# Two batches of a feed-forward network put behind attention as seven block products, with q/k copies on GpSimd and half of the output evictions on ScalarE

## The chip, the core and the metric

The kernel runs on one core of a Trainium2 chip. The metric is the device time of one execution in microseconds. Before the change it is 324.69 us, the median of three runs (324.67 to 325.06). One more execution was taken with the hardware profiler; its span, from the first to the last instruction, is 322.9 us, and TensorE's granted clock was 1.000 throughout.

The engines are named as the profile names them: PE is TensorE (matrix products), PEld its loading of weights, DVE is VectorE, ACT is ScalarE, POOL is GpSimd, SP is the engine that mostly issues transfers. Each engine works through its own queue in order, and an instruction that must wait holds up what stands behind it on that queue. SBUF is the on-chip memory that all engines work on; PSUM holds the results of matrix products, in eight banks of 512 float32 columns for each of 128 partitions.

## What is computed

Attention with one extra term in the softmax's denominator, over 8 batches, 12 heads, 448 positions and a head size of 64, and behind it a feed-forward network with three up-projections, of which the elementwise maximum is taken:

```python
def _attn_ref(q, k, v):                       # each (8, 12, 448, 64)
    scale = 1.0 / np.sqrt(q.shape[-1])
    scores = scale * np.matmul(q, k.transpose(0, 1, 3, 2))
    m = np.max(scores, axis=-1, keepdims=True)
    e = np.exp(scores - m)
    attn = e / (np.sum(e, axis=-1, keepdims=True) + np.exp(-m) + 1e-09)
    return np.matmul(attn, v)

def _moe_ref(x, w1, w2, w3, w_out):           # x (3584, 768), weights (768, 768)
    h = np.maximum(np.maximum(x @ w1, x @ w2), x @ w3)
    return h @ w_out
```

x is attention's result with the heads of one position side by side, so each of its 3584 rows belongs to one position of one batch.

## The kernel before

**Attention.** The 12 heads of a batch are taken in three groups of four, which makes 24 groups, numbered 0 to 23. In a group, four heads lie in the four 64x64 quarters of TensorE and are worked on side by side, so four matmuls of 64x64 run in the time of one. One group is

- seven "score" units (`visit`): four matmuls of 448 columns each into a pair of PSUM banks (tile "stp"), then one exponential on ScalarE over 896 columns into tile "eT";
- six additions on VectorE that sum the exponentials of the seven units (`sum_e`, tile "eS");
- one denominator (`den_group`): four matmuls with ones, then a logarithm on ScalarE into "lnd", and `recip_group`, an exponential of its negative into "rb";
- one product with v (`num_group`): 28 matmuls into a pair of banks (tile "av"), and `norm_group`, two multiplications on VectorE that write x transposed into the tile "xT" of the batch.

Three pairs of PSUM banks are shared in turn by scores, denominator and products in the early part; two in the later part.

**Loads and transposes.** GpSimd issues the loads of q, k and v, and in the later part each load waits for a score matmul so that loads are spread (`load_behind`). TensorE needs q and k transposed. For groups 0 to 7 it transposes them itself. From group 8 on, two VectorE copies (`copy_qk`, line 190) bring k and q of group i+2 into one tile "qk16", and one transposing transfer on SP's queue (`dma_transpose`) makes "qkT".

**Feed-forward.** It is cut into pieces. An up piece (`up_piece`) is one of 6 column blocks of one of 3 up-projections for one batch: 6 sets of four matmuls of 64x64 by 448 columns (line 758). VectorE then copies the result to "hT" (first projection) or takes the maximum with what is there. An output piece (`out_piece`) is one of 7 tiles of 128 rows of two batches, and one of 2 halves of 384 columns: 6 sets by 384 columns; VectorE scales it into an output tile "o_sb" (line 542), and after the second half two stores go out on SP's queue, 192 KB each. The batches' pieces stand in a list; `step` issues the next set, up to three pieces being worked on together, in a ring of four single PSUM banks.

**Order.** From group 7 on the order of TensorE's work is written out: for each group a list (`ORDER`) of score units (U), denominator (D) and product (N) with a weight each, and after every item so many `step`s as `rate` and the weight say. `batch_done(b)` adds the pieces of batch b once its x is there and sets the rate. The last four pieces are held back each time (`HELD`) to fill the stretch until the next batch is ready. A piece is taken up only when what it reads is written. After group 23 what is left of the pieces is worked off, which here is a good part of batches 6 and 7.

Names that the prediction's steps use: "set" is four matmuls of 64x64 side by side; "group 22" is the last but one; "the first av group" is the first whose product stands as 28 matmuls on line 322, "the last" is group 23's.

Of the kernel before, what the change touches and what calls it, by code (L numbers as in the profile page):

```python
# [10 lines left out]
FP32 = mybir.dt.float32  # L11
FP16 = mybir.dt.float16
AF = mybir.ActivationFunctionType
ALU = mybir.AluOpType
# [8 lines left out]
def kernel(  # L23
# [33 lines left out]
    )  # L57

    cpool = ctx.enter_context(tc.tile_pool(name="const", bufs=1))
    ld_pool = ctx.enter_context(tc.tile_pool(name="ld", bufs=5))  # L60
    p16_pool = ctx.enter_context(tc.tile_pool(name="p16", bufs=3))
    att_pool = ctx.enter_context(tc.tile_pool(name="att", bufs=4))
    e_pool = ctx.enter_context(tc.tile_pool(name="e", bufs=3))
    small = ctx.enter_context(tc.tile_pool(name="small", bufs=2))
    xt_pool = ctx.enter_context(tc.tile_pool(name="xt", bufs=2))
    ht_pool = ctx.enter_context(tc.tile_pool(name="ht", bufs=2))
    out_pool = ctx.enter_context(tc.tile_pool(name="outp", bufs=6))

    ps1 = ctx.enter_context(tc.tile_pool(name="ps1", bufs=2, space=bass.MemoryType.PSUM))
    ps2 = ctx.enter_context(tc.tile_pool(name="ps2", bufs=1, space=bass.MemoryType.PSUM))
    third = ExitStack()
    ps3 = third.enter_context(tc.tile_pool(name="ps3", bufs=1, space=bass.MemoryType.PSUM))
    turn = [0]
# [61 lines left out]
            reason="spreads the loads",  # L137
        )

    first_k = cpool.tile([128, 2, NJ, D], FP32, name="first_k")  # L140
    load_half(nc.sync, first_k, "k", 0, 0)
    load_half(nc.scalar, first_k, "k", 0, 1)
    load_group(0, "q")
# [22 lines left out]
                )  # L166
    w_sb = [cpool.tile([128, NDC, DFF], MMDT, name=f"w{i}") for i in range(4)]
    wout_sb = w_sb[3]


    def load_weight(i, f0=0, f1=DFF):
# [14 lines left out]
    def copy_qk(i, n):  # L186
        st = state.setdefault(i, {})
        if n == 0:
            st["qk16"] = p16_pool.tile([128, 2, NJ, 2, D], MMDT, tag="qk16", name="qk16")
        nc.vector.tensor_copy(  # L190
            out=st["qk16"][:, n].rearrange("p j s d -> p s j d"), in_=raw[i]["kq"[n]]
        )

# [43 lines left out]


    def first_group():
        k16 = p16_pool.tile([128, NJ, 2, D], MMDT, tag="k16", name="k16", bufs=1)  # L240
        qkT = att_pool.tile([128, 2, NJ, 128], MMDT, tag="qkT", name="qkT")
        state[0] = {"qkT": qkT}
        cuts = (((0, 4), (0, 3)), ((4, NJ), (3, NJ)))
        for (k0, k1), _ in cuts:
            nc.vector.tensor_copy(
                out=k16[:, k0:k1].rearrange("p j s d -> p s j d"), in_=first_k[:, :, k0:k1]
            )
        for (k0, k1), (q0, q1) in cuts:
            nk = k1 - k0
            trT = single("trT", (NJ, 128), MMDT)  # L250
            for j in range(k0, k1):
                nc.tensor.transpose(
                    out=trT[:, j - k0, :], in_=k16[:, j].rearrange("p s d -> p (s d)"),
                    identity=ident16,
                )
            for j in range(q0, q1):
                transpose_slots(trT[:, nk + j - q0, :], raw[0]["q"][:, :, j])
            nc.vector.tensor_copy(out=qkT[:, 0, k0:k1], in_=trT[:, 0:nk])
            nc.vector.tensor_copy(out=qkT[:, 1, q0:q1], in_=trT[:, nk:NJ])
# [70 lines left out]
    def den_group(i):  # L330
        st = state[i]
        dps = double("den")
        av_tiles(
            [dps[:, r, 0:S] for r in range(2)],
            lambda r, c: ones16[half(r)],
            lambda r, c: st["eS"][half(r), c],
            True,
            True,
        )
        st["lnd"] = small.tile([128, 2, S], FP32, tag="lnd", name="lnd")  # L340
        nc.scalar.activation(  # L341
            out=st["lnd"], in_=dps[:, :, 0:S], func=AF.Ln, bias=1.0 / EDIV
        )

    def recip_group(i):
        st = state[i]
        st["rb"] = small.tile([128, 2, S], FP32, tag="rb", name="rb")
        nc.scalar.activation(  # L348
            out=st["rb"], in_=st.pop("lnd"), func=AF.Exp, bias=math.log(LAMBDA), scale=-1.0
        )  # L350

    def num_group(i, in_pair=True):
# [66 lines left out]
    def den_part(i, part):  # L419
        st = state[i]  # L420
        q0, q1 = PARTS[part]
        nq = (q1 - q0) * KC
        eT = st["eT", part]
        dps = double("den")
        terms = [eT[:, j] for j in range(NJ)]
        if "eP" in st:
            eP, n = st.pop("eP")
            terms = [eP[:, 0], eP[:, 1]] + terms[n:]
        for n, e in enumerate(terms):
            av_tiles(  # L430
                [dps[:, r, 0:nq] for r in range(2)],
                lambda r, c: ones16[half(r)],
                lambda r, c: e[half(r), c],
                n == 0,
                n == len(terms) - 1,
            )
        lnd = small.tile([128, 2, S], FP32, tag="lnd", name="lnd")
        nc.scalar.activation(
            out=lnd[:, :, 0:nq], in_=dps[:, :, 0:nq], func=AF.Ln, bias=1.0 / EDIV
        )  # L440
        rb = small.tile([128, 2, S], FP32, tag="rb", name="rb")
        nc.scalar.activation(
            out=rb[:, :, 0:nq], in_=lnd[:, :, 0:nq], func=AF.Exp, bias=math.log(LAMBDA), scale=-1.0
        )
        st["rb", part] = rb

# [80 lines left out]
    def out_piece(bp, t, nh, bank=None, done=False):  # L527
        if nh == 0:
            outs[0] = out_pool.tile([128, DM], FP32, tag="o_sb", name="o_sb")
        o_sb = outs[0]  # L530
        op_ps = single("op_ps") if bank is None else bank
        for fc in range(0 if done else NFC):
            nc.tensor.matmul(  # L533
                out=op_ps[:, 0:NW],
                lhsT=hT[bp][:, fc, ts(t, 128)],
                rhs=wout_sb[:, fc, ts(nh, NW)],
                start=(fc == 0),
                stop=(fc == NFC - 1),
            )
        last = bp == B // 2 - 1 and t == NT - 1  # L540
        cut = nh * NW + (NW // 2 if last and nh == NH - 1 else NW)
        nc.vector.tensor_scalar(  # L542
            out=o_sb[:, nh * NW : cut],
            in0=op_ps[:, 0 : cut - nh * NW],
            scalar1=1.0 / LAMBDA,
            scalar2=None,
            op0=ALU.mult,
        )
        if cut < nh * NW + NW:
            nc.scalar.activation(  # L550
                out=o_sb[:, cut:DM], in_=op_ps[:, NW // 2 : NW], func=AF.Copy, scale=1.0 / LAMBDA
            )
        if last or nh == NH - 1:
            cols = ts(nh, NW) if last else slice(0, DM)
            for n in range(2):
                b, j = divmod(2 * t + n, NJ)
                b += 2 * bp
                rows = out[b * S : (b + 1) * S].rearrange("(p j) m -> j p m", j=NJ)
                eng = nc.scalar if last and n == 1 else nc.sync
                eng.dma_start(out=rows[j][:, cols], in_=o_sb[half(n), cols])  # L560
# [8 lines left out]
    def add_ups(b):  # L569
        for fc in range(NFC):  # L570
            for i in range(3):
                pieces.append((up_piece, (b, fc, i), NDC * (S + 6)))
# [132 lines left out]

    third.close()
    flush()
    single_pools.append(ctx.enter_context(tc.tile_pool(name="ps4", bufs=2, space=bass.MemoryType.PSUM)))
    pair_pools.pop()
    LAG = 2  # L710
    flow = []
# [126 lines left out]
    TOTAL = sum(w for _, _, w in ORDER)  # L838


    def batch_done(b):
        add_ups(b)
        last_batch[0] = b == B - 1
        pieces.extend(held)
        held.clear()
        add_out(b, *((0, 3) if b % 2 == 0 else (3, 7)))
        if b < B - 1:
            held.extend(pieces[-HELD:])
            del pieces[-HELD:]
        rate[0] = (left() - (SPARE if b < B - 2 else LAST)) / 3  # L850

    SPARE, LAST = 30, 50
    rate = [0]
    batch_done(1)
    after(9, sum_e, MID, 1)
    after(14, sum_e, MID, 2)
# [3 lines left out]
    for i in range(MID, NI + 1):  # L860
        for op, j, w in ORDER if i > MID else ORDER[4:]:
            if op == "U" and i < NI:
                mm = visit([(i, j)])
                n, name = ((2, "v"), (3, "k"), (3, "q"), (0, ""))[j // 2]
                if n > 0 and i + n < NI and i > MID:
                    load_behind(mm, i + n, name, j % 2)
                steps[0] += 1
                if j == 2:
                    recip_group(i - 1)
                if j > 0:  # L870
                    after({1: 9, 2: 14, 3: 20, 4: 9, 5: 9, 6: 9}[j], sum_e, i, j)
                if j == (9 if i == 7 else 3) and PE_TR <= i + 2 < NI:
                    for n_ in range(2):
                        copy_qk(i + 2, n_)
                    dma_transpose(i + 2)
# [16 lines left out]
            steps_for(rate[0] * w / TOTAL if i < NI else (8 if op == "D" else 0))  # L892
    while late or left() or count[1] < count[0]:
        step()


# [28 lines left out]
```

## Time and profile before

| | us |
|---|---|
| median of three runs | 324.69 |
| span of the profiled execution | 322.9 |
| TensorE busy | 308.2 (95%) |
| VectorE busy | 235.3 (73%) |
| ScalarE busy | 191.7 (59%) |
| GpSimd busy | 96.8 (30%) |
| feed-forward matmuls, line 758 | 246.0 in all |
| score exponentials, line 299, 147 of them | 132.8, 0.916 each |
| additions of exponentials, line 308, 126 of them | 78.0, 0.619 each |
| q/k copies, line 190, 32 of them | 12.4, 0.387 each |
| output evictions, line 542, 56 of them | 29.7, 0.550 each |
| end of the last attention product | 274.8 |
| end of the last matmul | 317.4 |

The busy time of TensorE is no measure of its limit: matmuls overlap, and a matmul that waits inside the pipeline counts as busy. So the number of matmuls between two points in the program's order, each at the time that undisturbed ones take, is set against the time that the trace shows between these points. The chain of waits, which follows the execution back from its end, is read in order of time: each line has the start in us, its length, the engine or transfer, the tile, the line and a count. In the groups of instructions the columns are: line, engine, operation, output<-input with partitions x columns and type, count | busy us, mean ns of one | idle time before them and what ended it. In the timeline they are: start, length, engine, line, operation, count, and in brackets the idle time before it.

### The profile page before, as it was taken

The numbers are of one execution on the slowest core, as the hardware profiler recorded it, in microseconds if no ns is written. First come the engines' busy times: TensorE is split into PE (matmuls) and PEld (weight loads), VectorE is DVE, ScalarE is ACT, GpSimd is POOL, SyncE is SP. The second block draws the span as 40 slices with busy tenths as digits, with TensorE's granted clock in tenths as the row PEclk, the third lists the DMA queues.
The fourth block names the chain that finished last, engine by engine and source line by source line (L and its number), as shares of the span: only waits on it lengthen the run. The fifth ranks groups of instructions, "written<-read, shape, count | busy, mean of one in ns | idle before, by whom it ended". The sixth has DMA issues, their size and how long they took to land.

```text
span 322.9 us, 14605 instructions
## 1 busy us (share of the span) xinstructions
PE 308.2 (95%) x6607; PEld 260.1 (81%) x6607; DVE 235.3 (73%) x443; ACT 191.7 (59%) x227; POOL 96.8 (30%) x166
## 2 busy tenths in 40 slices
PE   7669998999999999999999999999999999999993
PEld 6557676658998899988889877897787788887892
DVE  3446598998887878777769688878778777645652
ACT  2898859887786565575575685685576674000000
POOL 8947565840433132232222232232220000000000
PEclk9999999999999999999999999999999999999999
DMA  7999999999877975779969997899966500050046
GB/s 143 165 191 186 190 190 188 163 159 185 119 98 105 197 135 94 116 147 163 76 99 150 198 150 111 103 179 157 92 81 124 136 4 2 2 150 2 2 122 175
DMA packets 59517, 40.75 MB, mean 126 GB/s; under 512 B 32704, under 2 KB 56000, under 8 KB 59456
## 3 DMA queue, kind: packets, MB, share of 16 engines
q0 software_dynamic: 25344, 21.01, 48.1%
q1 hardware_dynamic: 33808, 18.39, 28.3%
q8 instruction: 51, 0.84, 1.1%
q10 hardware_dynamic: 304, 0.43, 0.5%
q14 instruction: 10, 0.08, 0.1%
HBM read 42.47 MB, written 11.01 MB: 166 GB/s over the span
## 4 chain that ended last, share of the span: by engine, by line
PE 79%; DMA 14%; POOL 3%; issue 1%; DVE 1%; ACT 0%; ACTq 0%; DVEq 0%; POOLq 0%
PE piece L758 59%; PE av L322 9%; PE stp L276 8%; DMA w<-in_moe_w_dram 7%; DMA ld_q<-in_q_dram 4%; DMA w<-in_moe_w_out_dram 2%; PE piece L533 2%; PE den L322 1%; PE piece L510 1%; DMA out_dram<-o_sb 1%; POOL w L180 1%; POOL w L181 1%; POOL ld_v L111 1%; POOL ld_q L111 1%; DVE eS L308 0%
## 5 line engine op out<-in xcount | busy, mean ns | idle before, releaser
L758 PE MATMUL piece<-xT,w 64*64 64x448 f16 x3024 | 177.7, 349 | 0.3 <-DVE xT L375 0.3
L299 ACT ACTIVATE eT<-stp 128x896 f16<-128x896 f32 x147 | 132.8, 916 | 65.9 <-PE stp L276 63.3
L758 PEld LDWEIGHTS <-w 64*64 64x64 f16 x3024 | 132.1, 107 | 21.2 <-issue 1.6
L276 PE MATMUL stp<-qkT 64*64 64x448 f16 (+2 forms) x756 | 71.3, 331 | 2.4 <-ACT eTp L394 0.8
L758 PE MATMUL piece<-w,hT 64*64 64x384 f16 x1224 | 68.3, 323 | 0.0
L308 DVE TENSOR_TENSOR eS<-eS,eT 128x896 f16<-128x896 f16 x105 | 65.0, 619 | 2.7 <-DVE eS L308 0.5
L499 DVE TENSOR_TENSOR hT<-hT,piece 128x448 f16<-128x448 f16 x84 | 51.9, 618 | 19.8 <-PE piece L758 16.8
L758 PEld LDWEIGHTS <-hT 64*64 64x64 f16 x1224 | 53.6, 107 | 4.4 <-issue 0.7
L111 POOL DMA_DIRECT2D ld_q<-in_q_dram x48 | 28.9, 606 | 60.3 <-PE piece L758 33.9
L111 POOL DMA_DIRECT2D ld_v<-in_v_dram x48 | 28.5, 599 | 47.7 <-PE stp L276 30.1
L276 PEld LDWEIGHTS <-qkT 64*64 64x64 f16 x756 | 32.1, 106 | 10.2 <-issue 5.5
L542 DVE TENSOR_SCALAR o_sb<-piece 128x384 f32<-128x384 f32 (+1 forms) x56 | 29.7, 550 | 13.4 <-PE piece L758 12.8
L497 DVE CAST hT<-piece 128x448 f16<-128x448 f32 x42 | 26.1, 621 | 14.4 <-PE piece L758 13.8
L111 POOL DMA_DIRECT2D ld_k<-in_k_dram x46 | 27.7, 609 | 27.5 <-PE piece L758 12.0
L322 PE MATMUL av<-eT,ld_v 64*64 64x448 f16 x588 | 33.3, 349 | 0.0
L322 PEld LDWEIGHTS <-ld_v 64*64 64x64 f16 x756 | 28.7, 107 | 4.2 <-issue 0.2
L375 DVE TENSOR_TENSOR xT<-av,rb 128x448 f16<-128x448 f32 x42 | 24.3, 619 | 9.0 <-PE av L322 8.8
L550 ACT ACTIVATE o_sb<-piece 128x192 f32<-128x192 f32 x1 | 0.3, 330 | 44.6 <-DMA out_dram<-o_sb 44.6
L510 PEld LDWEIGHTS <-w 128*128 128x128 f16 x216 | 18.8, 98 | 6.2 <-issue 4.1
L341 ACT ACTIVATE lnd<-den 128x896 f32<-128x896 f32 x21 | 19.3, 917 | 7.2 <-PE den L322 6.6
L394 ACT ACTIVATE eTp<-stp 128x768 f16<-128x768 f32 (+3 forms) x24 | 18.0, 821 | 7.1 <-PE stp L276 7.1
L348 ACT ACTIVATE rb<-lnd 128x896 f32<-128x896 f32 x21 | 20.0, 951 | 0.2
(50 smaller groups left out, 158.0 us busy)
## 6 DMA issues: line engine op xcount, KB each, us to landing
out_dram<-o_sb SPq DMA_DIRECT2D x54, 192.0 KB, 4.0
ld_q<-in_q_dram POOLq DMA_DIRECT2D x48, 112.0 KB, 4.3
ld_v<-in_v_dram POOLq DMA_DIRECT2D x48, 112.0 KB, 3.8
ld_k<-in_k_dram POOLq DMA_DIRECT2D x46, 112.0 KB, 4.2
w<-in_moe_w_dram POOLq DMA_DIRECT2D x6, 192.0 KB, 6.7
w<-in_moe_w_out_dram POOLq DMA_DIRECT2D x3, 384.0 KB, 7.6
w<-in_moe_w_dram POOLq DMA_DIRECT2D x2, 384.0 KB, 6.2
w<-in_moe_w_dram POOLq DMA_DIRECT2D x1, 576.0 KB, 8.3
```

Source lines behind the costliest of these rows:

```text
L111: return eng.dma_start(out=dst[hp * KC : hp * KC + KC].rearrange("p s j d -> p s (j d)"), in_=src[:, half_heads(name, hp)],)
L276: mm = nc.tensor.matmul(out=out[half(c), r], lhsT=qkT[half(r), 0, j, h], rhs=qkT[half(r), 1, q0:q1, h], start=True, stop=True,)
L299: nc.scalar.activation(out=st["eT"][:, j], in_=stp[:, :, 0:S], func=AF.Exp, scale=scale, bias=-math.log(EDIV))
L308: nc.vector.tensor_tensor(out=st["eS"], in0=st["eT"][:, 0] if j == 1 else st["eS"], in1=st["eT"][:, j], op=ALU.add,)
L322: nc.tensor.matmul(out=outs[r][half(c)], lhsT=weights(r, c), rhs=moving(r, c), start=start, stop=stop,)
L348: nc.scalar.activation(out=st["rb"], in_=st.pop("lnd"), func=AF.Exp, bias=math.log(LAMBDA), scale=-1.0)
L375: nc.vector.tensor_tensor(out=xT[b][:, 2 * g + r, :], in0=banks[r][:, 0:S], in1=state[i]["rb"][:, r], op=ALU.mult)
L497: nc.vector.tensor_copy(out=dst, in_=p_i[:, 0:S])
L499: nc.vector.tensor_tensor(out=dst, in0=dst, in1=p_i[:, 0:S], op=ALU.max)
L510: nc.tensor.matmul(out=p_i[:, ts(j, nq)], lhsT=w_sb[i][:, dc, ts(2 * fp + j, 128)], rhs=xT[b][:, dc, q0 * KC : q1 * KC], start=(dc == 0), ...
L542: nc.vector.tensor_scalar(out=o_sb[:, nh * NW : cut], in0=op_ps[:, 0 : cut - nh * NW], scalar1=1.0 / LAMBDA, scalar2=None, op0=ALU.mult,)
L758: nc.tensor.matmul(out=p["bank"][half(c), 0:w], lhsT=lhs(k, r, c), rhs=rhs(k, r), start=(r == p["first"] and k == 0), stop=(r != p["first" ...
```

## The change

- The pieces of batches 6 and 7 are no longer in the list. `batch_done` now handles batches 0 to 5 (`LATE = B - 2`), and the rate spreads what is left of them over all groups to come, but for 30 sets.
- When attention and those pieces are done, the pools of attention and all PSUM banks are given back, and a tail begins with eight single banks and full 128x128 matmuls. The two batches' rows and the halves of the contraction form 2x2 blocks, and so do each weight's halves. Each up-projection (9 units: 3 projections x 3 column blocks) and each output unit (3 units) is made of seven block products of three matmuls each, p1 to p7, in place of eight. Products accumulate in two banks, "a" and "s", and ScalarE copies or VectorE additions take intermediate sums out between them. The seventh tile of 128 rows of the pair, and four held pieces, are computed as before (`plain`).
- The block sums of the weights ("comb", four for each weight, 1152 columns) are subtractions on GpSimd: those of the first weight at the start of group 22, the others behind attention. The block sums of x ("sx", 1344 columns) and of h ("sh", 1152 columns) are four VectorE operations each.
- The q/k copies from group 11 on are on GpSimd.
- Half of the output evictions (the second 384 columns) are on ScalarE, but for the last tile.
- The logarithm is written straight into "rb" and the exponential is taken in place; the first k tiles come from the pool of "qk16"; "xT" has four buffers, not two, and "o_sb" five, not six.

```diff
-        nc.vector.tensor_copy(
+        eng = nc.gpsimd if i > 10 else nc.vector
+        eng.tensor_copy(
             out=st["qk16"][:, n].rearrange("p j s d -> p s j d"), in_=raw[i]["kq"[n]]
         )
...
-        nc.vector.tensor_scalar(
-            out=o_sb[:, nh * NW : cut],
...
+        if nh == 0 or last:
+            nc.vector.tensor_scalar(
+                out=o_sb[:, nh * NW : cut],
...
+        else:
+            nc.scalar.activation(
+                out=o_sb[:, NW:DM], in_=op_ps[:, 0:NW], func=AF.Copy, scale=1.0 / LAMBDA
+            )
...
+    LATE = B - 2
     def batch_done(b):
-        add_ups(b)
-        last_batch[0] = b == B - 1
...
+        if b < LATE:
+            add_ups(b)
+            last_batch[0] = b == LATE - 1
...
-        rate[0] = (left() - (SPARE if b < B - 2 else LAST)) / 3
+        coming = sum(NFC * 3 + (6 if x % 2 == 0 else 8) for x in range(b + 1, LATE))
+        steps_left = left() + NDC * (coming + (len(held) if b < LATE - 1 else 0))
+        rate[0] = (steps_left - LAST) / max(NI - max(3 * b + 3, MID) - 0.4, 1)
+    LAST = 30
...
+    def combine_weight(i):
+        w, t, m = w_sb[i], comb[i], DFF // 2
+        sub = ALU.subtract
+        b11, b12 = w[:, 0:3, 0:m], w[:, 0:3, m:DFF]
+        b21, b22 = w[:, 3:6, 0:m], w[:, 3:6, m:DFF]
+        for out_, in0, in1 in ((0, b12, b11), (1, b22, t[:, 0]), (2, b22, b12), (3, b21, t[:, 1])):
+            nc.gpsimd.tensor_tensor(out=t[:, out_], in0=in0, in1=in1, op=sub)
...
+                if j == 1 and i == NI - 2:
+                    combine_weight(0)
...
+    banks.close()
+    att.close()
+    tail = ctx.enter_context(tc.tile_pool(name="tail", bufs=1))
+    tps = ctx.enter_context(tc.tile_pool(name="tps", bufs=8, space=bass.MemoryType.PSUM))
+    for i in range(1, 4):
+        comb[i] = tail.tile([128, 4, 3, DFF // 2], MMDT, name=f"comb{i}")
+        combine_weight(i)
...
+    def combine_moving(name, a11, a12, a21, a22, n):
+        s = tail.tile([128, 4, 3, n], MMDT, name=name)
+        sub, add = ALU.subtract, ALU.add
+        for out_, in0, in1, op in (
+            (0, a21, a22, add),
+            (1, s[:, 0], a11, sub),
+            (2, a11, a21, sub),
+            (3, a12, s[:, 1], sub),
+        ):
+            nc.vector.tensor_tensor(out=s[:, out_], in0=in0, in1=in1, op=op)
+        return s
+    sx = combine_moving("sx", x1[:, 0:3], x1[:, 3:6], x2[:, 0:3], x2[:, 3:6], S)
...
+        def put(b, fc, out_of, bank, other=None):
+            dst = h_of[b][:, fc]
+            if other is None and i == 0:
+                nc.scalar.activation(out=dst, in_=bank, func=AF.Copy)
+            elif other is None:
+                nc.vector.tensor_tensor(out=dst, in0=dst, in1=bank, op=ALU.max)
+            elif i == 0:
+                nc.vector.tensor_tensor(out=dst, in0=other, in1=bank, op=ALU.add)
+            else:
+                nc.vector.tensor_tensor(out=out_of, in0=other, in1=bank, op=ALU.add)
...
+        def p1():
+            bank_of(u, "a")
+            copy("p1", product(u, "a", lambda k: w[:, k, c0], lambda k: x1[:, k], S, True))
+        def p2():
+            bank_of(u, "s")
+            bank = product(u, "s", lambda k: w[:, 3 + k, c0], lambda k: x1[:, 3 + k], S, True)
+            u["c"] = tail.tile([128, 3, S], MMDT, tag="c", name="c", bufs=3)
+            put(0, f, u["c"][:, 0], bank, u["p1"])
+            if i > 0:
+                dst = h_of[0][:, f]
+                nc.vector.tensor_tensor(out=dst, in0=dst, in1=u["c"][:, 0], op=ALU.max)
+        def p6():
+            copy("u2", product(u, "a", lambda k: t[:, 1, k, c0], lambda k: sx[:, 1, k], S, False))
+        def p7():
+            copy("p7", product(u, "s", lambda k: t[:, 2, k, c0], lambda k: sx[:, 2, k], S, True))
...
+        return [p1, p2, p6, p7, p5, p4, p3]
...
+    fill = [x for f, a, w in held for x in plain(*a)]
+    ups = [(i, f) for i in range(3) for f in range(3)]
+    for n in range(0, 8, 2):
+        in_turn(up_unit(*ups[n]), up_unit(*ups[n + 1]))
+    in_turn(up_unit(*ups[8]), fill)
+    sh[0] = combine_moving(
+        "sh", hp[:, 0:3, 0:NT3], hp[:, 3:6, 0:NT3], hp[:, 0:3, NT3 : 2 * NT3], hp[:, 3:6, NT3 : 2 * NT3], NT3
+    )
+    in_turn(out_unit(0), out_unit(1))
+    a = out_unit(2)
+    b = plain(B // 2 - 1, NT - 1, 0) + plain(B // 2 - 1, NT - 1, 1)
+    for x in (a[0], b[0], a[1], a[2], b[1], a[3], a[4], b[2], a[5], a[6], b[3]):
+        x()
```

`in_turn` issues the units' products alternately: p1 of both, p2 of both, and so on.

## The prediction

> **What bounds the kernel now.** I read the share of each engine over the span first (the page's slices; each digit is tenths of a slice of 8.1 us):
>
> ```profile
> PE   7669998999999999999999999999999999999993
> DVE  3446598998887878777769688878778777645652
> ACT  2898859887786565575575685685576674000000
> POOL 8947565840433132232222232232220000000000
> ```
>
> TensorE (PE) is nearly full from the fourth slice on; ScalarE (ACT) ends with attention, six slices before the end. But a busy TensorE can hide waits, so I took the chain of waits in order of time:
>
> ```profile
> 119.11 1.32 PE av L322 x28
> ...
> 132.16 1.32 PE av L322 x28
> ...
> 274.76 39.39 PE piece L758 x878
> ```
>
> 28 matmuls of 64x64 by 448 columns in 1.32 us are seven sets of four that run side by side: 0.189 us a set. The same division gives 0.1625 us for 384 columns (six in 0.97 us in the chain). I counted what stands on TensorE between one "av" and the next in the program's order and multiplied: 13.05 us between the two above, and the chain shows 132.16 - 119.11 = 13.05. From the end of the first av group (58.45 + 1.32 = 59.8) to the end of the last (274.8) the count gives 211.1 us and the trace 215.0, so 3.9 us are lost to waits, 0.3 to 0.6 in each group that holds output pieces and nothing in most others. After 274.8 the count gives 42.3 and TensorE ends at 317.45: 42.7. The last 5.45 us are eviction and stores. So matmul count sets this kernel, and a change is priced by counted matmuls plus new waits.
>
> The other durations, groups by form and the timeline:
>
> ```profile
> L308 DVE TENSOR_TENSOR eS<-eS,eT 128x896 f16<-128x896 f16 x105 | 65.0, 619 | 2.7 <-DVE eS L308 0.5 <-ACT eT L299 0.4
> L542 DVE TENSOR_SCALAR o_sb<-piece 128x384 f32<-128x384 f32 x55 | 29.5, 554 | 13.4 <-PE piece L758 12.8
> L394 ACT ACTIVATE eTp<-stp 128x384 f16<-128x384 f32 x3 | 1.5, 488 | 0.0
> L190 DVE COPY qk<-ld_q 128x896 f16<-128x896 f16 x16 | 6.2, 388 | 0.5 <-DMA ld_q<-in_q_dram 0.5
> masks.py:199 POOL TENSOR_SCALAR_AFFINE_SELECT ident<-ident 128x128 f16<-128x128 f16 x1 | 0.3, 287 | 0.1
> masks.py:197 POOL MEMSET ident<- 128x128 f16 x1 | 0.2, 231 | 0.0
> ```
> ```profile
> 114.01 0.62 DVE L308 TENSOR_TENSOR eS<-eS,eT 128x896 f16<-128x896 f16 x1
> 114.54 0.61 DVE L499 TENSOR_TENSOR hT<-hT,piece 128x448 f16<-128x448 f16 x1
> 115.07 0.62 DVE L497 CAST hT<-piece 128x448 f16<-128x448 f32 x1
> ```
> ```profile
> 52.06 2.54 ACT L299 ACTIVATE eT<-stp 128x896 f16<-128x896 f32 x3
> ```
>
> Queued VectorE (DVE) instructions of 0.62 us start every 0.53; three exponentials of 0.916 take 2.54, so 0.81 each. GpSimd (POOL) shows arithmetic on at most 128 columns, and never beside a busy VectorE.
>
> **The sum** is made against the span of 322.9; the median 324.69 lies 1.8 above it, and I add that at the end.
>
> **Seven products for eight: -6.6 us.** Two batches of up-projections were 36 pieces x 6 sets x 0.189 = 40.8; now nine units x 21 matmuls x 0.189 = 35.7 (full-array matmuls, one for each former set; six of 384 columns took 0.97, so the full array costs the same). Six of the pair's seven output tiles: 72 x 0.1625 = 11.7, now 63 x 0.1625 = 10.2. The program holds these counts, so the change does what it says.
>
> **Attention with less work between: +3.0.** Counted work from first to last av falls from 211.1 to 191.1, and what follows rises from 42.3 to 55.7. A group is now 9.6 to 11.2 us, not 9.6 to 13.05, with the same exponentials: 7 x 0.81 + 0.81 + 0.85 = 7.3 us of ScalarE, plus 0.39 for each output eviction put there (0.488 less the overlap). The heaviest group gets three of these, 8.5 of 9.8 us. They stand in a queue behind exponentials: a piece's bank is freed late by what is in front, up to 0.9. Some 16 such evictions: between 0 and 16 x 0.45 = 7; I take 3, under half, as banks rotate over four. VectorE keeps its load: per group some 16 x 0.53 = 8.5 of 11, as 18 x 0.53 + 0.6 of copies were 10.1 of 13.
>
> **The walk through the tail: +2.5.** Three waits can be worked out. At its start the first unit's bank needs the last attention piece evicted: 0.30 (ScalarE starts 0.49 after a score set of 0.19) + 0.49 = 0.8. Before the output products VectorE has a last maximum (0.62) and four sums of 1152 columns (1152/2/0.96 + 152 ns = 0.75 each, after the 619 ns of 896) in front of the eviction that frees bank "s": 0.3 + 0.6 + 3.0 + 0.55 = 4.5 against 3.4 of cover (seven products of 0.49): 1.0. In the last mixed unit a store on ScalarE's queue waits for VectorE and holds the p7 copy: 0.7. Bounds 0.8 (only the first) and 4. Within the units nothing queues: for 21 matmuls, 3.97 us, VectorE has five instructions of 0.53 and one of 0.30 (448 columns from two SBUF tiles, after the overlap), 3.0 in all, and ScalarE three copies of 0.45 (between the 488 ns of 384 columns and the 592 of 512, less the overlap).
>
> **Stores: +0.8.** Stores take 0.57 us each on SP's queue; about ten now come due in the last 7 us of matmuls, so the last goes out 3.0 after TensorE ends, where it was 2.25. Bounds 0 and 2.
>
> **At nothing.** The moved q/k copies stand on GpSimd's queue before loads of q and v that have a group or more of lead (10 us against 2.8), and transposes on SP's queue wait for them with two groups of lead; stores behind those land in 4.0, with five output tiles in the ring. If that cover were gone, 4 us of landing would show. The "lnd" tile, first_k and k16 only change place.
>
> **GpSimd beside VectorE: +9.1.** This is the unknown. A GpSimd subtraction of 1152 columns: from the two POOL rows, 1.0 to 1.5 ns a column, twice the upper if its two inputs come one after the other: 1.3 to 3.5 us. I take 1.8, the one-input row, the nearest. Copies of 896: 1.0 to 1.4. TensorE needs the last of twelve tail subtractions 48 us after attention, so up to 4.0 each they are in time. What no row shows is whether they and VectorE's operations on two SBUF tiles hold each other up. If not, the price is 0. If each excludes the other, the tail's four sums "sx" (1344 columns, 0.85 each) alternate with subtractions: 4 x (0.85 + 1.8) = 10.6 for 3.4, and the bank "s" of the first unit waits behind them: 6.6 after 0.6 of cover. In group 22 four subtractions take 7.2 us among six eS adds; up to 4 x 1.8 = 7.2 of delay less 2.4 of slack (10.0 - 7.6): 0 to 4.8, I take 2.5. Copies: two adds of a group wait up to 1.4, about the group's slack: 0 to 6 in all, I take 0. Exclusive: 9.1 at 1.8; 5 at 1.3; 25 at 3.5. Between ends 0 and 25 I take 9.1: exclusion, at the nearest row's speed.
>
> [...]
>
> **Sum:** 322.9 - 6.6 + 3.0 + 2.5 + 0.8 + 9.1 = 331.7, and 1.8: 333.5 us.
>
> **Rivals.**
> *A: no collision, savings eaten by waits.* The sum without 9.1: 322.6, 324.4 measured; 320.5 to 328.5 with the bounds above. For it: DMA issues on POOL of 0.59 us run beside eS adds that keep 0.62. Against: those read no wide tile.
> *B: faster, the saving comes through.* The new evictions hide as VectorE's did, collisions cost nothing, only the 0.8 at the tail's start stays: 322.9 - 6.6 + 0.8 = 317.1, 318.9 measured (317.5 to 321). For it: groups at 9.65 ran at their count, 9.65, with ScalarE at 7.3. Against: output groups lost 0.3 to 0.6 even on the emptier queue. It decides if sx sums stay near 0.85 back to back and no output eviction waits over 0.5.
> *C: GpSimd too slow for TensorE*, over 4.0 a subtraction: 12 x (5 - 4) = 12 us at 5, 337 with A's waits. Above both rows; it lies in the range.
>
> **How the numbers follow.** Forecast (exclusion, 329 to 349): 0.46. A: 0.28. B: 0.22. C: 0.04. About 0.2% (0.65 us) is what a measurement of this kernel can tell from no change. Faster: B whole and 0.10 of A = 0.32; same: 0.06 of A; slower: the rest, 0.62. The range: from inside B, 318, to 346, leaving out about 0.05 below and 0.1 above.
>
> **What would show it.** The sx sums in the tail: 0.85 apart (A, B) or some 2.6 (forecast). GpSimd subtractions: 1.3 to 3.5 us. Group 22's length: 10 or over 12. TensorE idle at the first unit's p7: none or some 6 us. Counted matmuls from tail start to end: 52 us. The forecast falls if VectorE keeps its 0.53 spacing beside GpSimd work.

## The result and the profile after

The change makes the kernel slower: 343.6 us median (342.77 to 345.36, four runs) against 324.88 (324.67 to 327.03, four runs), a ratio of 1.0575 with a 95% interval of 1.0527 to 1.0623. The profiled execution of the changed kernel has a span of 342.1 us, 19.2 above that of before. As before, a measured time lies some 1.7 us above its span.

The page of the changed kernel, engine shares in 40 slices (now of 8.55 us) and the granted clock:

```profile
PE   7779999989999999999998989997799938999992
DVE  3456688969796897689686786888878494888741
POOL 8867557432254345544454345459400699900000
PEclk9999999999999999999999999999899987999997
```

TensorE has holes that it did not have: one near the end of attention (the 77 in slices 28 and 29) and one early in the tail (the 3 in slice 33). GpSimd is at 9 there, and at the holes and behind them the granted clock falls, to 8 and 7 tenths in the last row's slices, where it was 1.00 throughout before. The same page's groups (busy, mean ns, idle before):

```profile
L311 DVE TENSOR_TENSOR eS<-eS,eT 128x896 f16<-128x896 f16 x105 | 80.9, 770 | 3.1 <-ACT eT L302 0.3
L875 POOL TENSOR_TENSOR comb<-w 128x1152 f16<-128x1152 f16 x8 | 21.0, 2630 | 25.3 <-PE av L325 25.3
```

The adds of exponentials, 619 ns before, now take 770 on average with the same shapes, and a subtraction on GpSimd takes 2.63 us (the other eight, which read "comb" too, 2.55). The timeline of the changed kernel at the tail's start, VectorE's sums "sx" (start, length):

```profile
272.53 1.25 DVE L943 TENSOR_TENSOR sx<-xT 128x1344 f16<-128x1344 f16 x1
273.82 2.91 DVE L943 TENSOR_TENSOR sx<-sx,xT 128x1344 f16<-128x1344 f16 x1
276.65 3.01 DVE L943 TENSOR_TENSOR sx<-xT 128x1344 f16<-128x1344 f16 x1
279.58 3.00 DVE L943 TENSOR_TENSOR sx<-xT,sx 128x1344 f16<-128x1344 f16 x1
282.51 1.14 DVE L983 TENSOR_TENSOR hT<-p,bank_s 128x448 f16<-128x448 f32 x2
```

and GpSimd's subtractions in the same stretch:

```profile
270.70 2.37 POOL L875 TENSOR_TENSOR comb<-w,comb 128x1152 f16<-128x1152 f16 x1
273.02 2.98 POOL L875 TENSOR_TENSOR comb<-w 128x1152 f16<-128x1152 f16 x1
275.97 2.97 POOL L875 TENSOR_TENSOR comb<-w,comb 128x1152 f16<-128x1152 f16 x1
```

They alternate: one sum, one subtraction, about every 2.9 us. The first subtraction shown was under way before any sum came and took 2.37 us; the next ones, beside sums, take 0.6 more. What TensorE made of it (in brackets the idle time before, and its releaser):

```profile
276.82 1.30 PE L957 MATMUL bank_a<-sx,comb 128*128 128x448 f16 x6 [1.58 <-POOL comb L875]
283.17 2.40 PE L957 MATMUL bank_s<-sx,comb 128*128 128x448 f16 x6 [5.05 <-DVE hT L983]
```

The first wait is put down to GpSimd, but the four block sums of that weight were all done by 242.99, some 34 us earlier; what ended at 276.73 was the second "sx" sum, which the same matmuls read. The second wait is the eviction that stands behind all four sums on VectorE's queue. And then six matmuls take 2.40 us, where six of the same shape in the line above take 1.30: the granted clock was 0.50 from 283.1 to 285.6 us and 1.00 from 276.8 to 278.2. The windows of the changed kernel (length, TensorE busy, granted clock, DMA share, GB/s) show where the clock fell:

```profile
240.00:245.00 5.00, 3.65 (x48) 0.75 0.02 3
...
275.00:283.00 8.00, 1.53 (x8) 0.81 0.11 35
283.00:300.00 17.00, 16.83 (x80) 0.89 0.00 0
```

The first of these is the other hole, in the group with the first four subtractions (group 22). VectorE and TensorE there:

```profile
235.59 5.17 DVE L311 TENSOR_TENSOR eS<-eS,eT 128x896 f16<-128x896 f16 x2
240.69 0.61 DVE L498 CAST hT<-piece 128x448 f16<-128x448 f32 x1
```
```profile
241.35 1.14 PE L766 MATMUL piece<-xT,w 64*64 64x448 f16 x20 [3.90 <-DVE hT L498]
```

Two adds took 5.17 us, the cast of a finished piece stood behind them, and the next piece waited 3.90 us for it. The group took 15.94 us between its av starts against 10.03 counted.

I split each span at three marks: the first av start of 28 matmuls, the last av start, and the end of the last matmul. "Counted" is the matmul count of the program at 0.189 and 0.1625 us a set.

| us | before | changed | counted, changed |
|---|---|---|---|
| to the first av | 58.3 | 57.6 | |
| first to last av (attention) | 215.0 | 209.1 | 191.1 |
| last av to last matmul (tail) | 44.2 | 68.7 | 57.0 |
| last matmul to the end | 5.45 | 6.7 | |

By the count, 6.6 us of matmuls are saved. Against that attention loses 18 us to waits where it lost 4, and the tail 11.7 where it lost 0.6.

### The profile page after: what moved, and what is told of

It reads as the page before. It is cut to its first block, busy times and chain, and to the rows that moved or that the text cites. A ratio compares the mean times of both kernels' runs of the same rounds, so it can differ in the third digit from the quotient of the medians.

```text
span 342.1 us, 12683 instructions
## 1 busy us (share of the span) xinstructions
PE 309.8 (91%) x5599; PEld 221.8 (65%) x5599; DVE 251.7 (74%) x410; ACT 221.3 (65%) x290; POOL 161.3 (47%) x208
## 5 line engine op out<-in xcount | busy, mean ns | idle before, releaser
L766 PE MATMUL piece<-xT,w 64*64 64x448 f16 x2160 | 136.0, 352 | 6.3 <-DVE hT L498 4.8
L766 PEld LDWEIGHTS <-w 64*64 64x64 f16 x2160 | 84.5, 108 | 30.4 <-issue 9.5
L311 DVE TENSOR_TENSOR eS<-eS,eT 128x896 f16<-128x896 f16 x105 | 80.9, 770 | 3.1 <-ACT eT L302 0.3
L766 PE MATMUL piece<-w,hT 64*64 64x384 f16 x792 | 49.9, 323 | 0.6 <-DVE hT L500 0.6
L500 DVE TENSOR_TENSOR hT<-hT,piece 128x448 f16<-128x448 f16 x60 | 37.0, 617 | 15.5 <-PE piece L766 13.7
L766 PEld LDWEIGHTS <-hT 64*64 64x64 f16 x792 | 34.0, 107 | 6.3 <-issue 1.1
L875 POOL TENSOR_TENSOR comb<-w 128x1152 f16<-128x1152 f16 x8 | 21.0, 2630 | 25.3 <-PE av L325 25.3
L957 PEld LDWEIGHTS <-comb 128*128 128x128 f16 x108 | 11.0, 102 | 18.1 <-issue 7.8
L344 ACT ACTIVATE rb<-den 128x896 f32<-128x896 f32 x21 | 19.3, 919 | 5.0 <-PE den L325 4.3
L875 POOL TENSOR_TENSOR comb<-w,comb 128x1152 f16<-128x1152 f16 x8 | 20.4, 2550 | 0.3
```

What stands on the lines that cost most here:

```text
L311: nc.vector.tensor_tensor(out=st["eS"], in0=st["eT"][:, 0] if j == 1 else st["eS"], in1=st["eT"][:, j], op=ALU.add,)
L344: nc.scalar.activation(out=st["rb"], in_=dps[:, :, 0:S], func=AF.Ln, bias=1.0 / EDIV)
L500: nc.vector.tensor_tensor(out=dst, in0=dst, in1=p_i[:, 0:S], op=ALU.max)
L766: nc.tensor.matmul(out=p["bank"][half(c), 0:w], lhsT=lhs(k, r, c), rhs=rhs(k, r), start=(r == p["first"] and k == 0), stop=(r != p["first" ...
L875: nc.gpsimd.tensor_tensor(out=t[:, out_], in0=in0, in1=in1, op=sub)
```

## The experiments

Theory E, from the forecast: a GpSimd instruction that reads SBUF and a VectorE instruction with two SBUF inputs hold each other up, and that makes most of the loss. Rival W: the loss comes from the new arrangement itself (thinner groups, evictions in ScalarE's queue, a tail with chains), and it stays when GpSimd is freed. Ratios are against the kernel before, each with its 95% interval.

**All block sums on VectorE.** The twelve tail subtractions go between the tail's products, the first four are spread over groups 19 to 22:

```diff
-            nc.gpsimd.tensor_tensor(out=t[:, out_], in0=in0, in1=in1, op=sub)
+        nc.vector.tensor_tensor(out=t[:, out_], in0=in0, in1=in1, op=ALU.subtract)
```

> The changed kernel with all sixteen block sums of the weights on VectorE in place of GpSimd (the first weight's four spread over groups 19 to 22, the others between the tail's products), GpSimd left with loads and q/k copies. Theory E (a GpSimd subtraction and a VectorE operation on two SBUF tiles exclude each other): the 5.9 us that group 22 lost and the 6.6 us that TensorE waited behind the sx sums go, and with them the matmuls at half clock behind these waits, some 3 us: 343.6 - 15.5 = 328, between 326 and 331; the sx sums stand 0.8 to 0.9 us apart, and no granted clock under 0.98 after attention. Rival W (the tail's waits come from the order of its seven products, whoever forms the sums): above 338, with a wait of some 5 us left before the first unit's p7.

331.47 us, 1.0227 [1.0186, 1.0268]: half a microsecond above E's range of 326 to 331, and far from W's 338. The same sums in this run's timeline:

```profile
268.47 0.86 DVE L941 TENSOR_TENSOR sx<-xT 128x1344 f16<-128x1344 f16 x1
269.36 0.86 DVE L941 TENSOR_TENSOR sx<-sx,xT 128x1344 f16<-128x1344 f16 x1
270.14 0.85 DVE L941 TENSOR_TENSOR sx<-xT 128x1344 f16<-128x1344 f16 x1
...
272.74 0.75 DVE L874 TENSOR_TENSOR comb<-w 128x1152 f16<-128x1152 f16 x1
```

A sum takes 0.86 where it took 3.0, the tail takes 60.5 us in place of 68.7, the group that had lost 5.9 us takes 10.88, and the granted clock is 1.00 in every window from 200 us to the last matmul. A subtraction takes VectorE 0.75 us, a third of GpSimd's 2.37.

**Only the copies, or only the evictions, back on VectorE.**

```diff
-        eng = nc.gpsimd if i > 10 else nc.vector
+        eng = nc.vector
```

> The changed kernel with the q/k copies back on VectorE, all else kept. If the copies' exclusion costs what attention lost beyond the forecast outside group 22 (12 us lost against 3.9 before and 3 forecast for ScalarE, so 5 us): 338 to 340. If VectorE gains nothing because it does the two copies of 0.39 itself in place of waiting 0.94 for two: 342.5 to 344.5.

> The changed kernel with all output pieces' evictions back on VectorE. If waiting behind exponentials on ScalarE's queue holds banks (theory Q): 340 to 341.5, a gain of 2 to 3.5 us, in the groups that hold output pieces. If not: 342.5 to 345.

344.12 us, 1.0611 [1.056, 1.0662], and 346.06 us, 1.0696 [1.064, 1.0751]: neither gains alone. The first lies in the second of its two expected ranges, but not for the reason given with it: attention's other groups together became 3 us shorter, and the group with the first four subtractions took 18.26 us in place of 15.94. There the two copies on VectorE, 0.39 us each elsewhere, took 1.30 and 2.54 beside the subtractions (their means over the whole run rose from 0.386 and 0.388 us before to 0.448 and 0.536), and a score unit waited 5.70 us for a norm behind them on VectorE's queue. The second lies above both of its expected ranges: attention is 1.5 us shorter and the tail 3.0 longer than in the changed kernel, where the first sx wait grew from 1.58 to 2.93 us; the rest of it is not explained.

**Sums, copies and evictions all on VectorE**, so that only the late batches and the seven products are left of the change:

> All three together: seven products, but block sums, q/k copies and output evictions on VectorE. Theory E with additive parts: 324.9 - 6.6 of matmuls + 3.3 of waits and stores in the tail + 0 to 3 of VectorE load = 321.5 to 325. Rival W: above 334. If VectorE has become the bound in attention (8.5 us of 11 and 0.6 of copies and 0.3 of evictions in a group, 85%): 326 to 330, with groups longer than their counted matmuls by 0.4 us or more each.

328.09 us, 1.0130 [1.0080, 1.0180]. Theory E with additive parts (321.5 to 325) missed this, and so did W; the time lies in the third range, which made VectorE the bound of attention. With no work moved to GpSimd or ScalarE the rest is still slower than before. The waits of TensorE in this run from 58 us to the last matmul (total, times, longest):

```profile
PE stp L279 <- DVE xT L377: 1.0, 3, 0.4
PE bank_a L950 <- DVE o_sb L543: 0.8, 1, 0.8
PE bank_s L950 <- DVE o_sb L1044: 0.7, 1, 0.7
PE piece L761 <- DVE o_sb L543: 0.6, 1, 0.6
...
PE bank_s L950 <- ACT p L1037: 0.4, 1, 0.4
...
PE bank_a L950 <- DVE sh L936: 0.3, 1, 0.3
```

Many small ones, 5.8 us in the eleven of the whole view, where the same view of the kernel before has two with 0.5. In attention (199.5, 8.4 over the count) the longest sum is that of score units which wait for a bank that VectorE's norms free, 1.0; all that the view lists there is 3.0 of the 8.4, so what most of that loss waits for isn't shown, nor that VectorE is its bound. In the tail, 61.9 against 57.0, it is the start and the walk into the output products. The end takes 6.9.

**Collision by itself: four subtractions, or four memsets, in the kernel before.** Both go into group 22 and into a tile that nothing reads; the rest is the kernel before.

```diff
+                if j == 1 and i == NI - 2:
+                    for n in range(4):
+                        nc.gpsimd.tensor_tensor(
+                            out=spare[:, n % 2], in0=w_sb[0][:, 0:3, 384:768],
+                            in1=w_sb[0][:, 0:3, 0:384], op=ALU.subtract
+                        )
```
```diff
+                        nc.gpsimd.memset(spare[:, n % 2], 0.0)
```

> The kernel before, with four GpSimd subtractions (128x1152 f16 from two SBUF inputs, into a tile that nothing reads) added in group 22, where the change puts its first four; nothing else differs and TensorE has the longer groups of before. E (exclusion: a VectorE operation with two SBUF inputs and a GpSimd operation that reads SBUF hold each other up): the eS adds of that group take 2 to 3 us in place of 0.62, the group goes from 10.8 to 14 to 17 us between its av starts, the whole 3 to 6 us longer: 327 to 330 us against 324. N (GpSimd's time does no harm by itself; what hurt was the change's thinner groups): adds stay at 0.62, time within 0.7 us of before.

> The same place and the same tile, but four GpSimd memsets, which write 128x1152 f16 and read nothing. E as stated (reads of GpSimd collide): adds stay at 0.62 us, time within 0.7 us of before. A rival R (any long GpSimd instruction, or its place on GpSimd's queue in front of loads, costs the time): 2 to 5 us longer, with adds lengthened or loads late.

With subtractions 334.48 us, 1.0286 [1.0249, 1.0323]; with memsets 325.67 us, 1.0033 [1.0005, 1.0062]. The timeline of the run with subtractions, GpSimd and VectorE:

```profile
237.70 9.31 POOL L873 TENSOR_TENSOR spare<-w 128x1152 f16<-128x1152 f16 x4
```
```profile
237.94 9.55 DVE L309 TENSOR_TENSOR eS<-eT 128x896 f16<-128x896 f16 x1
247.42 0.61 DVE L498 CAST hT<-piece 128x448 f16<-128x448 f32 x1
```

One add that takes 0.62 elsewhere took 9.55: it started 0.24 us after the first subtraction and ended 0.48 after the last. The cast behind it, which TensorE needed, could not start. The price was 9.7 us, not the 3 to 6 that E had said, because the add was held over all four; in the changed kernel the two alternate. Why they alternate there and not here no run tells. The windows of TensorE in this run:

```profile
240.00:245.00 5.00, 0.00 (x0) 0.88 0.00 0
245.00:250.00 5.00, 1.91 (x24) 0.50 0.01 3
250.00:255.00 5.00, 5.00 (x73) 0.60 0.49 93
```

TensorE stood for 8.55 us and then worked at a granted clock of 0.50. The run with memsets, GpSimd and VectorE:

```profile
241.40 4.07 POOL L873 MEMSET spare<- 128x1152 f16 x4
```
```profile
241.66 0.62 DVE L309 TENSOR_TENSOR eS<-eT 128x896 f16<-128x896 f16 x1
...
243.46 2.26 DVE L191 COPY qk<-ld_k 128x896 f16<-128x896 f16 x1
245.64 0.37 DVE L191 COPY qk<-ld_q 128x896 f16<-128x896 f16 x1
```

The same add beside GpSimd's memsets keeps its 0.62. So the add was held by the subtractions, which read SBUF, and not by the memsets, which only write; GpSimd's being at work was not enough. A plain copy, however, one input and 0.39 us elsewhere, took 2.26 beside the memsets and ended 0.25 us after the last of them. What sets the copy apart from the add the trace doesn't show. The run is 0.9 us above the one before, a little more than the 0.7 that E allowed.

**What the copies and the evictions cost once the sums are gone.** Sums and copies on VectorE, the evictions as in the change:

> Block sums and q/k copies on VectorE, half the output evictions left on ScalarE as the change has them: against the run with all three on VectorE (328.1) it prices the evictions, against the run with only the sums moved (331.5) it prices the copies. Q (my forecast's term: evictions queued behind exponentials hold banks): 330 to 332, that is 2 to 4 above 328.1. X (the copies beside VectorE's adds make the 3.4 between those runs, the evictions on ScalarE even relieve VectorE): 326.5 to 328.5, with attention at most 199.5 from first to last av.

328.56 us, 1.0113 [1.0074, 1.0151]: at X's upper bound and below Q. Half the evictions on ScalarE cost nothing in the whole against the run with all three moved. X's other sign failed, though: attention takes 201.5 in place of at most 199.5, with waits of 0.9 and 0.6 us that such evictions end, which is Q's mechanism, and the tail 60.3 in place of 61.9 makes up for it. What lies between this run and the one with only the sums moved (1.0227) is the copies: 1.1%, 3.7 us. The groups by form, first of the run with copies on GpSimd, then of this one (busy, mean ns):

```profile
L311 DVE TENSOR_TENSOR eS<-eS,eT 128x896 f16<-128x896 f16 x105 | 76.1, 724 | 2.9 <-ACT eT L302 0.3
```
```profile
L311 DVE TENSOR_TENSOR eS<-eS,eT 128x896 f16<-128x896 f16 x105 | 65.0, 619 | 2.8 <-ACT eT L302 0.3
```

The copies alone lengthen the adds by 11.1 us in all. To see whether only thin groups suffer from that, the copies alone in the kernel before:

> The kernel before with only its q/k copies moved to GpSimd from unit 11 on, as the change does it. T (the copies cost time only where groups are thin): eS adds beside a copy grow from 0.62 to as much as 1.9 us, their mean from 0.619 to some 0.72, and the groups of 12 to 13 us cover it: within 1 us of before. D (the copies delay what TensorE waits for in any group): 2 to 3.5 us longer, as between the two seven-product runs that differ in the copies alone (331.5 and 328.6).

327.47 us, 1.0120 [1.0084, 1.0156]: D, a little above its range, and not T, though the adds' mean, 0.713, is as T had it. The copies cost 3.9 us in the thick groups too; 3.3 of it lies in attention (218.3 for 215.0). TensorE has no wait of its own for a load or a transpose in this run, so it isn't that the copies hold up the loads behind them on GpSimd's queue. One place in this run's timeline:

```profile
239.67 0.94 POOL L191 COPY qk<-ld_k 128x896 f16<-128x896 f16 x1
240.54 0.94 POOL L191 COPY qk<-ld_q 128x896 f16<-128x896 f16 x1
```
```profile
239.93 2.04 DVE L309 TENSOR_TENSOR eS<-eT 128x896 f16<-128x896 f16 x1
241.89 0.61 DVE L498 CAST hT<-piece 128x448 f16<-128x448 f32 x1
```

The add, 0.62 us elsewhere, took 2.04 and ended 0.49 after the second copy, and the cast behind the add is one that TensorE waited 0.95 us for. The two groups around this place take 25.0 us in place of 23.3. The VectorE copies that were saved took 0.39 us each.

**The move without the seven products.** The last two batches behind attention with everything on VectorE, but as eight plain products:

```diff
+    ups = [(b, fc, i) for b in (LATE, LATE + 1) for fc in range(NFC) for i in range(3)]
+    for n, a in enumerate(ups):
+        whole_up(*a)
```

> The last two batches put behind attention as in the run of 328.1, but with the eight plain products in place of seven, and so with no block sums. It separates the move from the products. My sum says the move alone costs what attention loses (8.4 for 3.9, so +4.5) and 0.8 at the tail's start, and that seven products give 6.6 of matmuls less some 2.5 of waits and 1.5 at the end: 328 to 331 here, attention within 0.5 us of 199.5, last matmul 62.3 to 63.5 after the last av, end 5.4 after it. If seven products gave their full 6.6, this run would take 334.5.

328.05 us, 1.0129 [1.0103, 1.0154], the same as with seven (1.0130). The profiled execution was one of the longer ones (330.28 measured, span 328.5); its parts are 199.8 for attention, 65.7 for the tail (counted 63.6) and 4.8 for the end. With seven products the tail is 61.9, 3.8 less and not 6.6, and the end 6.9, 2.1 more. As the profiled execution with eight lies 2.2 us above its median, the 3.8 may be too much. So the seven products are worth at most 2 us here, and nothing that the medians show. The expected 328 to 331 was met with parts that were not those expected: 62.3 to 63.5 for the tail and 5.4 for the end. Both runs hold the change's smaller moves of buffers as well; these weren't tried apart.

**The late stores.** Half of them on GpSimd's queue, and the last tile's first store off ScalarE's:

```diff
-            nc.sync.dma_start(out=rows[j][:, n0:n1], in_=o[half(n), n0:n1])
+            eng = nc.gpsimd if n == 1 else nc.sync
+            eng.dma_start(out=rows[j][:, n0:n1], in_=o[half(n), n0:n1])
```

> All three on VectorE as in the run of 328.1, and half of the late stores issued by GpSimd's queue in place of SP's, the last tile's first half not on ScalarE's queue. S (the end of 7.0 us after the last matmul is late stores, and one store on ScalarE's queue holds the last unit's p7): the end shrinks to 5 to 5.7 us and the 0.4 wait for the p7 copy stays or goes with it: 326 to 327. Rival P (stores are limited by the transfers themselves, not by the issuing queue): 327.7 to 328.5, unchanged.

329.2 us, 1.0128 [1.0085, 1.0172]: no gain, as P said, but the trace doesn't bear P out. The 0.4 us wait in the last unit is gone. Stores now take 3.1 us (SP) and 4.1 (GpSimd) to land where they took 2.7, with the transfer engines nine tenths busy and more over the last 5 us of matmuls. The transfers from 300 us on in slices of 0.75 us, first with all stores on SP's queue, then with half of them on GpSimd's:

```profile
DMA  0002980019800000048979887988999700000000
DMA  0002980019800000049999999899971000000000
```

The last transfer ends 5.4 us after the last matmul in the first run (324.4 of a span of 325.9) and 4.5 us after it in the second (323.0 of 327.0): the stores do come out sooner. But the second span goes on for 4.0 us behind its last transfer, with no engine at work, where the first goes on for 1.5 and the kernel before for 1.5. That stretch takes the gain back; what it waits for the trace doesn't show, and only this run issues late stores on GpSimd's queue.

**Another spread over attention.**

```diff
-        ("N", 0, 2.2),
-        ("U", 4, 8),
+        ("N", 0, 3.7),
+        ("U", 4, 6.5),
...
-    LAST = 30
+    LAST = 23
```

> All three groups of work on VectorE (the run of 328.1), with the feed-forward pieces spread otherwise over attention: more steps after the numerators (3.7 for 2.2) and fewer after the unit behind them (6.5 for 8), and 23 steps left for the end in place of 30. H (attention's loss of 8.4 us against the count is a matter of where the filling work stands): first to last av 197.5 to 198.5 in place of 199.5, whole 325.5 to 327. K (the loss comes from shorter groups as such): 327.5 to 329.

327.2 us, 1.0104 [1.0066, 1.0143], attention 199.7. The time lies between the two expectations and its interval reaches into both, so the time settles nothing. The sign that H gave for attention, 197.5 to 198.5, did not come, in the one execution that was profiled. None of the versions tried beats the kernel before.

## Why the prediction was right and wrong

The direction and the mechanism were right: slower, as GpSimd's instructions and VectorE's two-input operations held each other up (an add of 0.62 us took 9.55 beside four subtractions, and a subtraction of 2.37 up to 2.98 beside the sums). The size was not: 333.5 forecast, 343.6 measured, a change of 18.7 us where 8.8 was forecast. Of the 10 us missed, 6 lie in the collision term, which put 9.1 where 15.0 came, and 4 in what is left without it. The prices, from run to run, as steps of the ratio times 324 us; a step's own uncertainty is near 2 us:

| step | forecast | measured |
|---|---|---|
| late batches, seven products, all on VectorE | -0.3 | +4.2 (1.0130) |
| half the evictions on ScalarE | in the 3.0 for attention | -0.5 (1.0113) |
| q/k copies on GpSimd | 0 | +3.7 (1.0227) |
| block sums on GpSimd | 9.1 | +11.3 (1.0575) |

The last two steps hold in this order only: with the block sums still on GpSimd, taking the copies back gained nothing (1.0611 against 1.0575). Their sum, 15.0, doesn't depend on the order.

**"GpSimd beside VectorE: +9.1" is the term that failed most, and it measured 15.0.** No row of the kernel before shows the exclusion that it rests on; to count on it was my estimate, and the runs show it. It had three parts.
- "6.6 behind the sx sums" came out as 1.58 + 5.05 = 6.63 us of waits. That the two agree is luck: the price of 1.8 a subtraction, set from a row of 128 columns, was too low (2.37 alone, 2.97 beside a sum), the first sum waited for only part of a subtraction, and the forecast had one wait where there were two.
- "2.5 in group 22" came out as 3.90 of wait and 5.06 of time (15.94 against 10.88 with the sums on VectorE). Three of the six adds were held, by up to a subtraction each (they took 2.59, 2.48 and some 1.7 us in place of 0.62), and the slack taken off the sum wasn't there.
- "Copies: ... I take 0" came out as 3.7 in this kernel and 3.9 in the kernel before. I set the adds' delay against the slack of a group. But the adds at the group's end are not all that TensorE waited for: in the place shown above it waited 0.95 us for an eviction that stood behind a held add on VectorE's queue.

What the sum had no term for is the clock after a wait: 0.75 over 5 us, 0.91 over the next 5 and 0.89 over 17 us in the tail cost, by estimate, 5 x 0.25 + 5 x 0.09 + 17 x 0.11 = 3.6 us. They are part of the 15.0.

**"Attention with less work between: +3.0" left out its larger part.** Attention loses 8.4 of its count with everything on VectorE, 3.9 before: 4.5 that have nothing to do with ScalarE. The queue on ScalarE, from which I argued, adds 2.0 there (201.5 for 199.5), which the tail gives back, so it has no price in the median. That the 4.5 come with the move of the last two batches, and its moves of buffers, and not with the seven products, the run with eight products shows (199.8). Whether the pieces are missing as filling is argued, not shown: a wider spread didn't cure it, and which dependency matters most isn't settled.

**"The walk through the tail: +2.5" was short.** The named waits are there with about their sizes: 0.56 and 0.79 at the start (0.8 forecast), 0.32 and 0.65 before the output products (1.0), 0.41 in the last unit (0.7). That is 2.7; the tail with everything on VectorE still loses 4.9 against 0.6 before, +4.3, and the cause of what the view of waits doesn't list (1.6) stays open. A sum of 1152 columns, put at 0.75, took 0.75 to 0.76; in the kernel before, additions of two f16 inputs in SBUF took 0.548 us at 768 columns and 0.686 at 1024, a slope that gives 0.755.

**"Stores: +0.8" measured 1.5** with everything on VectorE (6.9 for 5.45; 1.3 in the changed kernel). The last store's issue ends 3.6 us after the last matmul, not 3.0 (321.99 + 0.56 against 318.99), because the four in front of it took 0.78 us each and not 0.57; from there to the end it is 3.3, as before (3.2).

**"Seven products for eight: -6.6" is right as a count and wrong as a gain.** Over eight products in the same place they bring at most 3.8 in the tail and give back 2.1 at the end.

Of the rivals, A is what stands once GpSimd is out of it: 324.4 forecast, 328.1 to 328.6 found, at the upper bound of its 320.5 to 328.5. B fell on both of its conditions: the sums stood 2.9 us apart, and evictions on ScalarE ended waits of 0.9 and 0.6. C (whose sum gives 336.4, not 337) did not occur: a subtraction took at most 2.98, and TensorE waited for no "comb" in the tail but in the 1.58 shown above, which the second sx sum ended.

## What to carry to other kernels

GpSimd was no free helper beside a busy VectorE: a copy of 0.39 us on VectorE became 0.94 on GpSimd and made an add of 0.62 take up to 2.04, and a subtraction of 0.75 became 2.4 to 3.0 that held sums of 0.86 for as long. Price such a move by what stands behind the held instruction on VectorE's queue, not by the slack of the held instruction. And saved matmuls need not be worth their count: 6.6 us of them showed nothing in the median, as waits and late stores took their place. Test the bare move first, as the eight-product run did, before the saving is built.

## What the runs showed of the hardware

Some waits of TensorE cost more than their length. In the changed kernel waits of 3.90 and 5.05 us were followed by granted clocks of 0.75 and 0.89, as means of windows of 5 and 17 us, and six matmuls took 2.40 us in place of 1.30; after 8.55 us of standing the clock was 0.50. Behind the wait of 1.58 us six matmuls still took 1.30. In the run with everything on VectorE, with no wait above 0.8 us, the clock from 200 us to the last matmul stayed at 1.00.

GpSimd's instructions took 2.37 us (subtraction without a VectorE sum beside it, 1152 columns, f16), 0.94 (copy, 896 columns, even while it held an add) and 1.08 (memset, 1152 columns). And a VectorE instruction was held across four GpSimd instructions (9.55 us) or two (2.04), not only one.
